# A planner's longer assumed landings, an earlier release, a second stack buffer, and a paced first attention

## The chip, the cores and the metric

The kernel runs on one core of a Trainium2 chip. The metric is the device time of one execution in microseconds (us); several runs give a median. A core has TensorE (PE, matrix products on a 128 x 128 array), VectorE (DVE), ScalarE (ACT), GpSimd (POOL) and SyncE (SP, which issues most DMAs here). Each engine takes its instructions in the order in which the program lists them, and engines wait for each other through semaphores.

## The reference

For each of 4 batches with N = 12480 rows of C = 128, 32 learned rows `I` attend to the batch, and the batch then attends to the 32 results. A feed-forward layer with a leaky ReLU follows on all 49920 rows.

```python
h = mab(I, x)                       # 32 rows per batch: the first attention
y = mab(x, h)                       # every row of x attends to h: the second attention
# mab(q, kv): s = scale * q @ kv.T; a = softmax(s); return a @ kv
t = y @ w_in                        # 128 -> 2048
g = maximum(0.01 * t, t)
out = g @ w_out                     # 2048 -> 128
```

## The kernel before

**Tiles.** A batch is cut into six full groups of 2048 rows and a remainder of 192 (`GROUPS`, remainder `RG`). A full group gives four tiles of 512 rows; the remainders of two batches make one pair tile of 384, which stands after the first four tiles of batches 1 and 3 (`PAIR_AT`). There are 98 tiles. The first two and the last are written in a fixed order; the 95 between (`work`) are planned.

**What a tile needs.** The second attention of a row is a vector `a` of 32 weights, so `y @ w_in` is `a @ (h @ w_in)`, and the kernel keeps `h @ w_in` (`hw`) instead of `y`. All operands of the feed-forward part are split into a high and a low part, and three products of parts stand for one exact one. A tile has 16 chunks of 128 hidden columns. Per chunk there are three first products of 32 rows of the array (`a` times `hw`), a ReLU on ScalarE (`ghi`), the low part on VectorE or, in its far form, on GpSimd (`glo`), and three second products in four row groups, all of the latter through `quarter` (L988). Products of four row groups run beside each other. The linear part of the leaky ReLU is added in chunk 13 (`LINEAR`), where `A4`, the tile's `a`, is read for the last time; the four partial sums are gathered and added after chunk 15 (`gather`).

**How `a` gets there.** `second(b, g)` makes the second attention of a group: scores on the array, then transpose and maximum (DVE), subtraction (POOL), exponential (ACT), sums (DVE), product (POOL) and a last transpose (DVE, L837) into `aT`. It runs for one group after another, in the order 0, 1, remainder, 2 to 5, with at most four full groups ahead. `stack` takes a group's `aT`, writes its high part with ACT (L856) and its low part with POOL (L863) into the one buffer `both`, and copies it with DMAs (L878) into the `A4` buffers of its four tiles, four DMAs of 128 KB for each (24 small ones for a pair tile). There are three `A4` buffers.

**The next batch.** When the first product of a batch's first tile is planned, `begin` starts the first attention of the next batch: `first_scores` (loads of x by 32 x 32 blocks, `xc`, 16 DMAs a group; transposes; scores, L372; `running` keeps a running maximum, L406) and `first_values` (loads of rows, `xr`, four DMAs a group; products, L535). Sums (L605) and the summary `h` (L624) follow, then `expand_weights` (L752). Batch 1's begins earlier, in the fixed part, with its loads and its remainder.

**What sets the order.** From `quads[0] = True` (L1183) on, a planner writes the instruction order. It keeps a clock per engine and a time per row group, adds assumed costs (`RELU`, `LOW`, `QUARTER`) and, for what a DMA brings, `LANDED` = 2300 ns after its issue, and emits whatever could start first by these numbers. The lanes (stack, stores, second attention, values, scores) ask for an engine and a time. On PE a lane waits until it is 9 us old (`OLD`), or until two are ready and one is 3 us old, or until the rows would be idle; on the other engines a lane gives way to feed-forward work until it is 15 us late (`PATIENCE`). First products may run at most ten chunks ahead (`GB`). None of this changes what waits on the chip, only the order.

Of the kernel before, what the change touches and what calls it, by code (L numbers as in the profile page):

```python
# [9 lines left out]
F32 = mybir.dt.float32  # L10
F32R = mybir.dt.float32r
# [8 lines left out]
def induced_attention_then_leaky_ffn(  # L20
# [63 lines left out]
    QUICK = 2  # L84
    TURN = 4
    A4_BUFS = 3
    XR = 9
    GB = 10
    SLOT = 868.0
    QUARTER = 231.6  # L90
    SIGNAL = 35.0
    DRAINED = 200.0
    TURNED = 200.0
    LANDED = 2300.0
    RELU, LOW, COPIED, ADDED, BLOCKS = 599.0, 690.0, 585.0, 685.0, 700.0
    FAR_HIGH, FAR_LOW, FAR_SUM = 611.0, 1291.0, 1291.0
    EARLY, PREFER, YIELDING, PATIENCE = 1200.0, 0.0, 200.0, 15000.0
    OLD, PAIRED, IDLE, HURRY, TOGETHER = 9000.0, 3000.0, 300.0, 9000.0, 3
    LINEAR = NF - 3
    debt = [0]  # L100

    const = ctx.enter_context(tc.tile_pool(name="const", bufs=1))
# [237 lines left out]
    def load_rows(b, g, q):  # L340

        _, J, K = GROUPS[g]
        n = min(K, 4)
        t = sb.tile([P, 4, C], F32, tag="xr", name="xr", bufs=XR)
        src = rows_of(b, g).rearrange("(p k) c -> p k c", k=K)
        nc.sync.dma_start(t[: 32 * J, :n, :], src[:, 4 * q : 4 * q + n, :])  # L346
        xr[b, g, q] = t
        landed[b, g, q] = spent(SP, 490.0) + LANDED

    def load_blocks(b, g, j0, nj):  # L350

# [103 lines left out]
    def first_scores(b):  # L455
# [12 lines left out]
            more()  # L468
        if not quads[0]:
            yield from idle(4)  # L470
        for g in [RG, *range(RG)]:
            _, J, K = GROUPS[g]
            w = 32 * K
            if g == RG:
                xT[b, g] = t = sb.tile([P, J, w], F32, tag="xTr", name="xTr", bufs=2)
            else:
                yield from until(lambda: len(ring) < RING)
                ring.add((b, g))
                xT[b, g] = t = sb.tile([P, J, w], F32, tag="xT", name="xT", bufs=RING)
            at = 0.0  # L480
            for j in range(J):
                if g == RG:
                    if j:
                        continue
                    blk, at = blocks[RG, 0, 3]
                    yield from new(DVE, at)
                    nc.vector.transpose(
                        t.rearrange("p j w -> p (j w)"),
                        blk[:, : J * K, :].rearrange("p n c -> p (n c)"),
                    )  # L490
                else:
                    blk, at = blocks[g, j - j % 2, 2]
                    yield from new(DVE, at)
                    blk = blk[:, (j % 2) * K : (j % 2 + 1) * K, :]
                    nc.vector.transpose(t[:, j, :], blk.rearrange("p n c -> p (n c)"))  # L495
                at = spent(DVE, BLOCKS, at)
                yield from old(HEAVY)
                if j % 2 or g == RG:
                    yield from new(SP, at)
                    more()  # L500
            yield from new(PE, at)
            sp = aux_ps("s1_ps")
            for j in range(J):
                columns_product(sp, indT, b, g, j)
            at = on_array("c", 875.0 if g != RG else 120.0, at, taken[0])
            if quads[0]:
                rest = running(b, g, sp, at)
                for got in rest:
                    if got[0] == PE:
                        break  # L510
                    yield got
                middles.append(carried(got, rest))
            else:
                yield from running(b, g, sp, at)
                yield from old()
# [260 lines left out]

    def second(b, g, eng=None):
        eng = eng or nc.gpsimd
        yield from until(lambda: g == RG or sum(q != RG for _, q in aT) < 4)
        if (b, g) != (0, 0):  # L780
            yield from new(PE, landed.get((b, "h"), 0.0))
        hT = hw[b][0]
# [59 lines left out]
    def stack(tiles_, eng=None):  # L842
# [3 lines left out]
        for _, parts in tiles_:  # L846
            for b, g, *_ in parts:
                if (b, g) not in at:
                    at[b, g] = sum(32 * GROUPS[q][2] for _, q in at)
        when = max(landed.get("both", 0.0), *(landed.get((b, g, "aT"), 0.0) for b, g in at))  # L850
        yield from new(ACT, when)
        both = sb.tile([P, 2, TOK], F32R, tag="both", name="both", bufs=1)
        ahi, alo = both[:, 0, :], both[:, 1, :]
        for (b, g), o in at.items():
            _, J, K = GROUPS[g]
# [12 lines left out]
        yield from old()  # L868
        for t, parts in tiles_:
            yield from until(lambda: len(A4) < A4_BUFS)  # L870
            a4 = sb.tile([P, 2, TOK], F32R, tag="A4", name="A4", bufs=A4_BUFS)
            to = 0
            for b, g, js in parts:
                w, o = 32 * GROUPS[g][2], at[b, g]
                for j in js:
                    yield from new(SP, when)
                    for r in range(4):
                        nc.sync.dma_start(  # L878
                            a4[32 * r : 32 * r + 32, :, to : to + w].bitcast(F32),
                            both[32 * j : 32 * j + 32, :, o : o + w].bitcast(F32),  # L880
                        )
                        landed["A", t] = landed["both"] = spent(SP, 640.0, when) + LANDED
                    to += w
                    yield from old()
            A4[t] = a4
# [3 lines left out]
    def quick(t):  # L889
# [11 lines left out]
        mx = sb.tile([P, 4], F32, tag="mx", name="qmx")  # L901
        nc.vector.tensor_reduce(out=mx, in_=sv, op=ALU.max, axis=AX.X)
        if not qys:
            qys.append(sb.tile([P, QUICK, 4, M], F32, tag="both", name="qy", bufs=1))
        y = qys[0][:, t]
        nc.vector.tensor_tensor(
            out=y, in0=sv, in1=mx.unsqueeze(2).broadcast_to([P, 4, M]), op=ALU.subtract
# [194 lines left out]
    with tc.manual_schedule():  # L1102
# [134 lines left out]
        def gather(t, r, ready):  # L1237
# [30 lines left out]
                add(ACT, ready, COPIED, copied, lambda: (t, 0) in parts_of)  # L1268
            else:
                add(ACT, ready, COPIED, copied, lambda: not parts_used[0])  # L1270
            if r == 3:
                del A4[t]

        def products(t, f, r):
            parts, n = spans(t)
# [60 lines left out]
        def go(r, kind, start):  # L1336
# [37 lines left out]
            if last:  # L1374
                product_of[r] = 0
                turn_of[r] += 1
                if min(turn_of) > i:
                    del live[t, f]
                if f == NF - 1:
                    gather(t, r, at)  # L1380

# [130 lines left out]
```

## Time and profile before

| | us |
|---|---|
| runs | 1601.34, 1604.66, 1604.69 |
| median of the runs | 1604.66 |
| profiled execution: time | 1606.44 |
| profiled execution: span | 1604.7 |
| PE busy | 1565.6 |
| DVE, ACT, POOL busy | 1084.6, 1080.4, 1179.3 |

The span is the time from the first to the last profiled instruction; about 1.7 us lie around it. The fixed part ends at about 100 us. Batch 1's first tile begins at about 452 us, batch 2's at about 855 us. PE counts as busy while any of its row groups runs, so the number of products in a stretch tells more than its busy time. The granted clock is the share of full speed that the array was given.

### The profile page before, as it was taken

Reading aid. Unit: us, or ns where it says so; the run is one execution under the profiler, and the core shown is the slowest. Engines: PE = TensorE matmul, PEld = TensorE weight load, DVE = VectorE, ACT = ScalarE, POOL = GpSimd, SP = SyncE. Lnnn points to the kernel's source line nnn. Section 1 sums busy time; section 2 is a strip of 40 time slices with the busy share of each in tenths; the row PEclk is TensorE's granted clock in tenths of the full one; section 3 lists DMA queues with packets and bytes.
Section 4 is the critical chain, followed back from the end, with each engine's and each line's share of the span. In section 5 each row is a group of like instructions: output and inputs, shape, how many; then the busy total and the mean of one; then the engine's idle time right before and its main releaser. Section 6 shows DMA issues by size and latency. Waiting matters only on the chain.

```text
span 1604.7 us, 60005 instructions
## 1 busy us (share of the span) xinstructions
PE 1565.6 (98%) x25047; PEld 1360.7 (85%) x25047; DVE 1084.6 (68%) x1914; ACT 1080.4 (67%) x1957; POOL 1179.3 (73%) x1227
## 2 busy tenths in 40 slices
PE   7989999999999999999999999999999999999998
PEld 5658878899997876889999877789898899999996
DVE  6667886665666867666666876566666677666665
ACT  6446657777775655667777566677777777777774
POOL 2028716999998255699999458999999957778773
PEclk9899999999999999999999999999999999999999
DMA  7155653223254557323234667233233233232231
GB/s 266 16 115 98 126 140 74 50 56 62 35 109 70 101 103 151 82 55 61 48 62 93 109 125 159 60 64 58 46 70 58 37 67 63 55 65 53 57 61 21
DMA packets 400704, 128.49 MB, mean 80 GB/s; under 512 B 373136, under 2 KB 375600, under 8 KB 400432
## 3 DMA queue, kind: packets, MB, share of 16 engines
q1 hardware_dynamic: 399328, 124.50, 38.7%
q8 instruction: 197, 3.23, 0.8%
q14 instruction: 75, 0.61, 0.1%
q10 hardware_dynamic: 1104, 0.15, 0.1%
HBM read 48.94 MB, written 25.56 MB: 46 GB/s over the span
## 4 chain that ended last, share of the span: by engine, by line
PE 89%; SPq 4%; DMA 4%; DVE 2%; issue 1%; ACT 1%; POOL 0%; ACTq 0%; DVEq 0%; POOLq 0%
PE bank L988 83%; PE bank L372 2%; DMA xr<-in_x_dram 2%; SPq L878 2%; SPq L357 1%; PE bank L1018 1%; PE bank L535 1%; DVE glo L978 1%; DMA raw<-in_moe_w_in_dram 1%; SPq L346 0%; DMA A<-both 0%; POOL glo L1218 0%; ACT ghi L975 0%; PE bank L406 0%; DMA out_dram<-osb 0%
## 5 line engine op out<-in xcount | busy, mean ns | idle before, releaser
L988 PE MATMUL bank<-ghi,w_hi 32*128 32x512 f32 (+1 forms) x6080 | 1221.3, 393 | 4.8 <-ACT ghi L975 4.8
L988 PE MATMUL bank<-ghi,w_lo 32*128 32x512 f32 (+1 forms) x6080 | 1214.6, 392 | 0.0
L988 PE MATMUL bank<-glo,w_hi 32*128 32x512 f32 (+1 forms) x6080 | 1213.7, 392 | 0.0
L988 PE MATMUL bank<-A,hwhi 32*128 32x512 f32 (+1 forms) x3394 | 1051.6, 392 | 9.1 <-ACT g L975 3.6
L978 DVE SCALAR_TENSOR_TENSOR glo<-bank,ghi 128x512 fp32r<-128x512 f32 (+1 forms) x1052 | 697.3, 682 | 362.9 <-ACT ghi L975 345.3
L988 PEld LDWEIGHTS bank<-ghi,w_hi 32*128 32x128 f32 x6080 | 775.4, 184 | 42.9 <-ACT ghi L975 6.0
L988 PEld LDWEIGHTS bank<-glo,w_hi 32*128 32x128 f32 x6080 | 770.0, 184 | 35.2 <-issue 9.8
L988 PEld LDWEIGHTS bank<-ghi,w_lo 32*128 32x128 f32 x6080 | 773.4, 184 | 31.0 <-issue 5.8
L975 ACT ACTIVATE ghi<-bank 128x512 fp32r<-128x512 f32 (+1 forms) x1052 | 611.5, 598 | 217.4 <-PE bank L988 187.6
L1218 POOL TENSOR_TENSOR glo<-g,ghi 128x512 fp32r<-128x512 f32 (+1 forms) x516 | 668.1, 1295 | 41.3
L988 PE MATMUL bank<-A,hwlo 32*128 32x512 f32 (+1 forms) x1697 | 621.6, 390 | 0.0
L988 PEld LDWEIGHTS bank<-A,hwhi 32*128 32x128 f32 x3394 | 569.1, 184 | 38.1 <-DVE glo L978 7.3
L975 ACT ACTIVATE g<-bank 128x512 f32<-128x512 f32 (+1 forms) x516 | 308.6, 598 | 210.2 <-PE bank L988 174.3
L1216 POOL CAST ghi<-g 128x512 fp32r<-128x512 f32 (+1 forms) x516 | 316.4, 613 | 135.6 <-ACT g L975 96.0
L988 PEld LDWEIGHTS bank<-A,hwlo 32*128 32x128 f32 x1697 | 302.5, 184 | 6.2 <-issue 1.4
L1261 POOL TENSOR_TENSOR part<-part 128x512 f32<-128x512 f32 (+1 forms) x95 | 123.0, 1295 | 96.3 <-DVE part L1250 93.3
L1250 DVE TENSOR_TENSOR part<-bank,part 128x512 f32<-128x512 f32 (+1 forms) x190 | 129.8, 685 | 64.2 <-PE bank L988 42.8
L1244 ACT COPY part<-bank 128x512 f32<-128x512 f32 (+1 forms) x190 | 110.4, 583 | 18.1 <-PE bank L988 14.9
L1037 DVE STREAM_TRANSPOSE osb<-part 128x512 f32<-128x512 f32 (+1 forms) x95 | 66.6, 701 | 11.2 <-POOL part L1261 10.5
L826 POOL TENSOR_TENSOR y<-y,sm 128x512 f32<-128x512 f32 (+1 forms) x27 | 25.4, 941 | 32.0 <-DVE sm L822 17.2
L495 DVE STREAM_TRANSPOSE xT<-xc 128x512 f32<-128x512 f32 x72 | 47.4, 689 | 1.3 <-DMA xc<-in_x_dram 1.3
L863 POOL TENSOR_TENSOR both<-aT,both 128x512 fp32r<-128x512 f32 x24 | 31.1, 1296 | 20.9 <-DMA xr<-in_x_dram 12.5
(120 smaller groups left out, 632.5 us busy)
## 6 DMA issues: line engine op xcount, KB each, us to landing
A<-both SPq DMA_DIRECT2D x376, 128.0 KB, 2.4
xr<-in_x_dram SPq DMA_DIRECT2D x96, 256.0 KB, 4.6
out_dram<-osb SPq DMA_DIRECT2D x382, 64.0 KB, 2.2
xc<-in_x_dram SPq DMA_DIRECT2D x288, 64.0 KB, 2.9
raw<-in_moe_w_in_dram SPq DMA_DIRECT2D x4, 512.0 KB, 6.6
raw<-in_moe_w_out_dram SPq DMA_DIRECT2D x4, 512.0 KB, 6.8
A<-both SPq DMA_DIRECT2D x48, 16.0 KB, 1.8
out_dram<-osb SPq DMA_DIRECT2D x48, 8.0 KB, 1.8
```

What stands on the lines that cost most here:

```text
L372: nc.tensor.matmul(dst, lhsT, rhs, start=True, stop=True)
L495: nc.vector.transpose(t[:, j, :], blk.rearrange("p n c -> p (n c)"))
L878: nc.sync.dma_start(a4[32 * r : 32 * r + 32, :, to : to + w].bitcast(F32), both[32 * j : 32 * j + 32, :, o : o + w].bitcast(F32),)
L975: nc.scalar.activation(ghi[:, :n], ph[:, :n], AF.Relu)
L978: nc.vector.scalar_tensor_tensor(out=glo[:, :n], in0=ph[:, :n], scalar=0.0, in1=ghi[:, :n].bitcast(F32), op0=ALU.max, op1=ALU.subtract,)
L988: nc.tensor.matmul(dst, w[32 * r : 32 * r + 32], x[32 * r : 32 * r + 32], start=start, stop=stop, tile_position=(32 * r, 0),)
L1037: nc.vector.transpose(osb[:, :n], total[:, :n])
L1216: nc.gpsimd.tensor_copy(ghi[:, :n], g[:, :n])
L1218: nc.gpsimd.tensor_tensor(out=glo[:, :n], in0=g[:, :n], in1=ghi[:, :n].bitcast(F32), op=ALU.subtract)
L1244: nc.scalar.copy(part[:, :n], po[:, :n])
L1250: nc.vector.tensor_tensor(out=part[:, :n], in0=po[:, :n], in1=part[:, :n], op=ALU.add)
L1261: nc.gpsimd.tensor_tensor(out=total[:, :n], in0=total[:, :n], in1=part[:, :n], op=ALU.add)
```

## The change

`LANDED` goes from 2300 to 3800 ns, with 3000 more for the row loads (`xr`). The slot of `A4` is given up when all row groups have passed chunk 13, instead of when the last partial sum is gathered, and a new load of `A4` is planned no earlier than that read. `both` gets a second buffer, and the planner's time for it is that of the stack before last. For the space, `xr` has 7 buffers instead of 9. In the first attention, group number n (the remainder is 0) is not started before n x 38 us after the beginning (`PACE`). In the planned part the second attention runs at most two full groups ahead instead of four (`STOCK`).

```diff
@@ -84,19 +84,20 @@
     QUICK = 2
     TURN = 4
     A4_BUFS = 3
-    XR = 9
+    XR = 7
     GB = 10
     SLOT = 868.0
     QUARTER = 231.6
     SIGNAL = 35.0
     DRAINED = 200.0
     TURNED = 200.0
-    LANDED = 2300.0
+    LANDED = 3800.0
     RELU, LOW, COPIED, ADDED, BLOCKS = 599.0, 690.0, 585.0, 685.0, 700.0
     FAR_HIGH, FAR_LOW, FAR_SUM = 611.0, 1291.0, 1291.0
     EARLY, PREFER, YIELDING, PATIENCE = 1200.0, 0.0, 200.0, 15000.0
     OLD, PAIRED, IDLE, HURRY, TOGETHER = 9000.0, 3000.0, 300.0, 9000.0, 3
     LINEAR = NF - 3
+    PACE, STOCK = 38000.0, 2
     debt = [0]
 
     const = ctx.enter_context(tc.tile_pool(name="const", bufs=1))
@@ -345,7 +346,7 @@
         src = rows_of(b, g).rearrange("(p k) c -> p k c", k=K)
         nc.sync.dma_start(t[: 32 * J, :n, :], src[:, 4 * q : 4 * q + n, :])
         xr[b, g, q] = t
-        landed[b, g, q] = spent(SP, 490.0) + LANDED
+        landed[b, g, q] = spent(SP, 490.0) + LANDED + 3000.0
 
     def load_blocks(b, g, j0, nj):
 
@@ -468,9 +469,11 @@
             more()
         if not quads[0]:
             yield from idle(4)
-        for g in [RG, *range(RG)]:
+        began = now[0]
+        for n, g in enumerate([RG, *range(RG)]):
             _, J, K = GROUPS[g]
             w = 32 * K
+            yield from until(lambda: not quads[0] or now[0] >= began + n * PACE)
             if g == RG:
                 xT[b, g] = t = sb.tile([P, J, w], F32, tag="xTr", name="xTr", bufs=2)
             else:
@@ -776,7 +779,7 @@
 
     def second(b, g, eng=None):
         eng = eng or nc.gpsimd
-        yield from until(lambda: g == RG or sum(q != RG for _, q in aT) < 4)
+        yield from until(lambda: g == RG or sum(q != RG for _, q in aT) < (STOCK if quads[0] else 4))
         if (b, g) != (0, 0):
             yield from new(PE, landed.get((b, "h"), 0.0))
         hT = hw[b][0]
@@ -847,9 +850,10 @@
             for b, g, *_ in parts:
                 if (b, g) not in at:
                     at[b, g] = sum(32 * GROUPS[q][2] for _, q in at)
-        when = max(landed.get("both", 0.0), *(landed.get((b, g, "aT"), 0.0) for b, g in at))
+        when = max(landed.get(("both", 1), 0.0), *(landed.get((b, g, "aT"), 0.0) for b, g in at))
         yield from new(ACT, when)
-        both = sb.tile([P, 2, TOK], F32R, tag="both", name="both", bufs=1)
+        landed["both", 1] = landed.get(("both", 0), 0.0)
+        both = sb.tile([P, 2, TOK], F32R, tag="both", name="both", bufs=2)
         ahi, alo = both[:, 0, :], both[:, 1, :]
         for (b, g), o in at.items():
             _, J, K = GROUPS[g]
@@ -868,6 +872,7 @@
         yield from old()
         for t, parts in tiles_:
             yield from until(lambda: len(A4) < A4_BUFS)
+            when = max(when, landed.get("A4", 0.0))
             a4 = sb.tile([P, 2, TOK], F32R, tag="A4", name="A4", bufs=A4_BUFS)
             to = 0
             for b, g, js in parts:
@@ -879,7 +884,7 @@
                             a4[32 * r : 32 * r + 32, :, to : to + w].bitcast(F32),
                             both[32 * j : 32 * j + 32, :, o : o + w].bitcast(F32),
                         )
-                        landed["A", t] = landed["both"] = spent(SP, 640.0, when) + LANDED
+                        landed["A", t] = landed["both", 0] = spent(SP, 640.0, when) + LANDED
                     to += w
                     yield from old()
             A4[t] = a4
@@ -901,7 +906,7 @@
         mx = sb.tile([P, 4], F32, tag="mx", name="qmx")
         nc.vector.tensor_reduce(out=mx, in_=sv, op=ALU.max, axis=AX.X)
         if not qys:
-            qys.append(sb.tile([P, QUICK, 4, M], F32, tag="both", name="qy", bufs=1))
+            qys.append(sb.tile([P, QUICK, 4, M], F32, tag="both", name="qy", bufs=2))
         y = qys[0][:, t]
         nc.vector.tensor_tensor(
             out=y, in0=sv, in1=mx.unsqueeze(2).broadcast_to([P, 4, M]), op=ALU.subtract
@@ -1268,8 +1273,6 @@
                 add(ACT, ready, COPIED, copied, lambda: (t, 0) in parts_of)
             else:
                 add(ACT, ready, COPIED, copied, lambda: not parts_used[0])
-            if r == 3:
-                del A4[t]
 
         def products(t, f, r):
             parts, n = spans(t)
@@ -1376,6 +1379,9 @@
                 turn_of[r] += 1
                 if min(turn_of) > i:
                     del live[t, f]
+                    if f == LINEAR:
+                        del A4[t]
+                        landed["A4"] = at
                 if f == NF - 1:
                     gather(t, r, at)
 
```

## Rows read from the trace of the kernel before

**Rows 1.** The page's engine totals: busy us (share of the span) xinstructions.

```profile
PE 1565.6 (98%) x25047; PEld 1360.7 (85%) x25047; DVE 1084.6 (68%) x1914; ACT 1080.4 (67%) x1957; POOL 1179.3 (73%) x1227
```

**Rows 2.** L988 on PE, quiet stretches: length, PE busy (xproducts), granted clock, DMA share, GB/s.

```profile
1320.00:1340.00 20.00, 20.00 (x348) 1.00 0.19 37
...
1160.00:1180.00 20.00, 19.07 (x329) 1.00 0.42 80
```

**Rows 3.** The same view for the four holes, and one piece of the second.

```profile
104.00:116.00 12.00, 7.71 (x76) 0.72 0.63 126
564.00:576.00 12.00, 8.37 (x96) 0.72 0.30 59
632.00:644.00 12.00, 6.33 (x72) 0.72 0.87 219
956.00:964.00 8.00, 2.87 (x32) 0.79 0.87 163
568.00:572.00 4.00, 3.04 (x28) 0.50 0.12 19
```

**Rows 4.** The same view for two longer stretches; then L372 and L535 in one.

```profile
480.00:520.00 40.00, 35.19 (x572) 1.00 0.42 70
200.00:260.00 60.00, 53.44 (x819) 1.00 0.49 119
...
200.00:260.00 60.00, 3.20 (x24) 1.00 0.49 119
...
200.00:260.00 60.00, 3.24 (x96) 1.00 0.49 119
```

**Rows 5.** Who waited for whom: us in total, times, longest.

```profile
ACT both L856 <- DMA out_dram<-osb: 14.0, 2, 9.6
ACT both L856 <- DMA A<-both: 12.5, 5, 5.0
```

**Rows 6.** Timelines of SyncE and of ScalarE: start, us, instruction [idle before it].

```profile
563.15 2.46 SPq L878 DMA_DIRECT2D A<-both  x4
...
567.79 0.62 ACT L856 CAST both<-aT 128x512 fp32r<-128x512 f32 x1 [4.42 <-DMA out_dram<-osb]
```

**Rows 7.** DMA issues by line: xcount, KB each, median us from issue to landing.

```profile
A<-both SPq DMA_DIRECT2D x376, 128.0 KB, 2.4
xr<-in_x_dram SPq DMA_DIRECT2D x96, 256.0 KB, 4.6
```

**Rows 8.** The chain of work that ended last: start, us, what.

```profile
132.90 0.99 PE bank L372 x8
...
222.92 1.07 PE bank L372 x8
...
277.85 0.42 PE bank L624 x2
282.08 0.99 PE bank L372 x8
...
632.72 4.54 DMA xr<-in_x_dram
...
1002.59 0.99 PE bank L372 x8
...
1035.68 0.42 PE bank L624 x2
```

**Rows 9.** Timeline of SyncE: start, us, issues.

```profile
499.85 16.96 SPq L878 DMA_DIRECT2D A<-both  x24
...
1274.27 18.34 SPq L878 DMA_DIRECT2D A<-both  x24
```

**Rows 10.** Timelines of VectorE and GpSimd in the second attention: start, us, instruction.

```profile
283.89 0.69 DVE L800 TENSOR_REDUCE mx<-y 128x16 f32<-128x512 f32 x1
...
320.50 1.04 POOL L826 TENSOR_TENSOR y<-y,sm 128x512 f32<-128x512 f32 x1
...
410.61 0.23 DVE L837 STREAM_TRANSPOSE aTr<-y 96x64 f32<-96x64 f32 x1
```

## Prediction, made before the change was run

> **What bounds the kernel now.** I read the engine totals first [rows 1]: TensorE is busy 98% of the span, so idle time elsewhere matters only where it reaches TensorE. "Busy" hides much, though: four row groups work side by side, and the engine counts as busy while one of them runs. So the second view is the number of feed-forward products (L988) by stretch. Undisturbed, the array starts 348 in 20 us [rows 2], 17.4 per us, or 57.5 ns each. A lone interruption (one attention score) leaves 329: 19 products, 1.1 us, against 0.99 us of its own work in the chain (the 132.90 row of [rows 8]); so the turn to another tiling costs about 0.1 us. Where far more is missing, the array starved.
>
> Four holes stand out [rows 3]. At 17.4 per us, 104 to 116 us should hold 209 products and has 76; 564 to 576 has 96 of 209; 632 to 644 has 72 of 209; 956 to 964 has 32 of 139. The granted clock shows that a hole costs twice: at 568 to 572, right after the array stood idle, it is 0.50, the lower of the two levels (1.2 against 2.4 GHz), and the products that do run take longer. Longer, thinner losses are in [rows 4]: 480 to 520 has 572 of 696, 200 to 260 has 819 of 1044, part of which is other array work.
>
> The third view, who waited for whom, gives the causes. ScalarE's copy into the stacked high part (L856) waited 12.5 us for the DMAs that read the previous stack and 14.0 us in two more waits put down to a store's landing [rows 5]. The timelines show that these two are the same wait: the four reads of the old stack are issued on SyncE from 563.15, and the copy starts at 567.79, just as the last can have landed [rows 6]; the store was only issued next. The ReLUs written behind the copy start only after it, and then the array. Holes 1 and 2 and the loss at 480 are this wait. Hole 3 is another: the array stands before the values of the first attention until rows of x have landed; the chain has 4.54 us of xr landing at 632.72 [rows 8]. Hole 4, at the same point of the next batch's burst, I take to be alike. The planner assumed 2.3 us after issue, and the median over the run is 4.6, against 2.4 for the A transfers [rows 7].
>
> **Two buffers for the stacked parts.** The copy then overwrites the stack before last, whose reads were issued a group of four tiles earlier. A tile is about 243 products, 14 us, so that is over 50 us old: the wait goes. What returns, missing products times 57.5 ns: hole 1, 133 products, 7.6 us, of which I take 6.0, because the hand-over to the planned part also has to fill the array's lead; hole 2, 113, 6.5 us, less 0.6 for a small interruption, 5.9; the loss at 480, 124, 7.1 us, less some 2.6 for the score, value and maximum work in it, 4.5. Sum 16.4 us. Next late at 480 is the pair tile itself, whose 24 small transfers take SyncE 16.96 us [rows 9]; the second such pair takes 18.34 us at 1274 and sits beside a quiet array, so I charge nothing for it unless the stack comes late (below). Paying with two xr buffers costs nothing: the first attention keeps at most five loads outstanding, and in the setup only the eighth weight tile comes to a slot that another one held, the first, which is read long before. Without that cover a load would wait one group, as it does at hole 3.
>
> **Longer assumed landings.** They only move instructions in the written order: values of the first attention go behind products that can run. Hole 3: 137 missing, 7.9 us, less 1.5 of its own values and maxima, 6.4 (values take 3.24 us for 96 products, 1.1 per group of 32 [rows 4]). Hole 4: 107, 6.2 us, less 1.1 of values, 5.1. Sum 11.5 us. The array gets other work in that time because the rows are then ordered 6.8 us after issue, beyond the median. For A the assumption grows by 1.5 us; nothing waits for it while three A buffers are in turn, so zero, with 0 to 1 us at the hand-over.
>
> The Trainium skill speaks against this part: "DMA: Bandwidth & Descriptors", section "Anatomy of one DMA — SWDGE (gpsimd) path", gives a DMA a constant 2.0 us plus its bytes over 436 GB/s, on another issuing path. By it 128 KB would take an estimated 2.3 us, 256 KB 2.6 us, the old assumption was right and this part would be worth nothing. The A transfers' median agrees; the xr median does not, and the measurement decides.
>
> **A let go at its last read.** The slot is free at the end of chunk 13, not 15, and a chunk of a tile is 14/16 = 0.9 us: its load is ordered 1.7 us earlier. Hidden, as the load has two tiles to land; zero.
>
> **Pacing of the first attention, stock of two.** Before, the five steps from the score at 132.90 to that at 222.92 came at 18 us each [rows 8]. An issue takes SyncE 0.62 us (4 in 2.46 us, [rows 6]) to 0.76 us (24 in 18.34 us, [rows 9]). A group has 16 xc and 4 xr loads, some 13 us, and a tile 4 A transfers and 4 stores, 5 us. At 18 us a group needs 13 + 6.5 us: SyncE is full. At 38 us it needs 13 + 14, 70%. So the bursts thin out, and of the thin losses part returns: 200 to 260 misses 225 products, 12.9 us, less 3.2 of scores, 3.2 of values and some 2 of maxima and turns, so 4 to 5 us. The third batch's burst has the same work in the same manner, so I double it and take half, 4.5 us; bounds 0 and 9. The cost: work that shared an interruption will stand alone more often. At 0.1 us a turn and some 20 more, 2 us (0 to 5).
>
> The pacing also **moves the end of each batch's first attention**, and this is the step that I trust least. The planned part starts at 100 us; the sixth full group may not start before 100 + 6 x 38 = 328. Transposes and the wait for the array bring its score to about 341, where it was 222.92. From the last score to the end of the summary (L624) it took 54.9 us in the first batch and 33.1 us in the third (1002.59 to 1035.68) [rows 8], so the summary comes at 374 to 396 instead of 278. Then the second attention runs one group after another, and each is held up at GpSimd, which is full of low parts, twice: from the maxima at 283.89 to the final product at 320.50 are 36.6 us [rows 10], in which GpSimd does only two steps of 1 us for it. That is some 15 us for each of the two, the planner's patience. The third group in line, the 192-row remainder that the pair tile needs, was finished at 410.61, 128.5 us after the first score of that chain at 282.08. Moved, it is finished at 374 + 4 + 128 = 506 to 528. The pair's transfers need 17 us more and then a landing, 525 to 547; before, they were issued from 499.85 to 516.81 and the array was just short of them. The array will be some 8 us ahead of the old times and has a lead of ten chunks, 9 us, so it runs dry at about 511 to 517. It would lack 8 to 36 us. But when it lacks products the low parts stop and GpSimd comes free, so one or two of the 15 us waits shrink; I take 8 us and 2 us of lower clock, 10. In the third batch the planned interval is about 25 us longer, and I charge 2. Bounds 0 and 40 in all.
>
> **Sum** against the profiled execution: 1606.44 us with a span of 1604.7. Returned: 16.4 + 11.5 + 4.5 = 32.4. Given back: 2 + 10 + 2 = 14. Net 18.4 us. The median of the runs shown is 1604.66, 0.1% under the profiled one; taken from it, 1586.3 us.
>
> **Rivals.** (1) The paced chain is in time: the second attention reaches the remainder sooner, and nothing is given back at the pair. Then 1586.3 - 12 = 1574; with all thin losses and the whole of hole 1 back as well, 1568. For it: the hold-up is the planner's choice and not GpSimd's own time of 2 us a group. Against: from 282 it met a full GpSimd, and the moved chain falls into the same kind of stretch. (2) The longer landings bring nothing: holes 3 and 4 are then a backlog in SyncE's queue, which the new order meets again. The 11.5 us stay lost, and 1598 results. Against: the last link before the values in the chain is a landing of 4.54 us, not an issue. The constant landing on the page of the Trainium skill named above would give the same time. (3) Slower: the late second attention costs at every pair its full waits. The mechanism is the 15 us waits at GpSimd; it decides from the point where the pair's two stalls pass 30 us together, that is, with the remainder finished at 528 and no easing: 36 + 8 of clock at the first, half of that at the second, 44 + 22 = 66 against the 30 returned: 1641; with some easing, about 1615. (4) The pacing gives back just what the waits return: 1602 to 1608. That the change does not do what it says is part of (2): the copy's wait can't stay, since its two releasers are reads of one buffer.
>
> **Chances.** Forecast (1579 to 1594) 0.48; (1) 0.22; (2) 0.12; (4) 0.07; (3) 0.11. Range 1567 to 1604: it leaves out (3) and the far ends, and takes in both bounds of the pair. The likeliest one's own range is 1579 to 1594. A measurement of this kernel can tell about 0.2%, 3.2 us. Faster by more 0.82, within 0.07, slower by more 0.11.
>
> **What would show it.** Right: no wait of L856 over 1 us; no xr landing in the chain at the first attention's values; 104 to 116 and 564 to 576 with over 170 products; SyncE with pauses in the bursts. For the pair: the array starved at about 505 to 530 with the wait put down to A, and the remainder's last transpose (L837) after 500. Wrong: the array full through that stretch (rival 1), or a hole at each batch's first tile, which would mean that even the first group of the second attention comes too late.

## The result and the profile after

The changed kernel takes **1584.32 us** (median of 4 runs, 1584.06 to 1585.30) against 1603.45 us (1601.34 to 1604.69) for the kernel before: ratio 0.9883, 95% interval 0.9866 to 0.9900, 19.1 us less. The forecast was 18.4 us less, 1586.3. The profiled span went from 1604.7 to 1582.3 us; 3 of these 22.4 us are there because the profiled run of before lay that far above its median. The mean granted clock rose from 0.986 to 0.994.

The sum came out nearly right, but not by its parts. The experiments show that the end of the waits for xr was credited to the wrong edit.

The engine totals of the page, which answer to [rows 1], and GpSimd's busy tenths in 40 slices of the span:

```profile
PE 1560.1 (99%) x25047; PEld 1357.9 (86%) x25047; DVE 1193.6 (75%) x2096; ACT 1080.0 (68%) x1957; POOL 840.7 (53%) x863
...
POOL 2127971566411399998311399977899843110100
```

The count on TensorE is the same. GpSimd lost 364 instructions and VectorE gained 182: 334 low parts are made on GpSimd where 516 were (L1223 against L1218), and the planner now gives the others to VectorE. Over the span VectorE is busy 75% and GpSimd 53%, so on average both have room for it.

Products (the quarter matmul, now L993) in the same windows as [rows 3] and [rows 4]: length, TensorE busy (xproducts), granted clock, DMA share, GB/s.

```profile
104.00:116.00 12.00, 9.40 (x116) 0.86 0.75 147
564.00:576.00 12.00, 9.82 (x162) 1.00 0.63 111
632.00:644.00 12.00, 11.07 (x192) 1.00 0.63 110
956.00:964.00 8.00, 8.00 (x144) 1.00 0.59 107
480.00:520.00 40.00, 38.38 (x666) 1.00 0.43 75
200.00:260.00 60.00, 56.72 (x934) 1.00 0.47 90
```

Holes 2, 3 and 4 are closed (162 for 96, 192 for 72, 144 for 32). Hole 1 is closed only in part: 116 where 76 were and 209 have room. At 480 the count flatters the change: the pair tile, whose products have 192 or 384 columns instead of 512, begins sooner, and 162 of the 666 products are such narrow ones, where 25 of the 572 were. Counted by columns it is 601 for 556, which is 2.6 us returned. Others of these windows flatter the change too, since paced attention work has moved out of them. A fairer count takes every stretch apart: the products started in it at 57.4 ns each (those of the pair tile by their columns), the spans of the interruptions by other array work, from the product before to the product after, and the rest, which is what the array missed. Undisturbed stretches show a rest of some 0.3 us in 20. Single rows move by up to 0.6 us with the side to which an interruption at an edge is counted; the sum does not.

| stretch, us | missed before | missed after | returned | forecast for it |
|---|---|---|---|---|
| 100 to 140 (hole 1) | 9.1 | 6.4 | 2.7 | 6.0 |
| 140 to 480 | 7.8 | 6.2 | 1.6 | 2.25 (pacing) |
| 480 to 680 (loss at 480, holes 2 and 3, first pair) | 18.3 + 4.1 standing at values | 9.4 | 13.0 | 16.8 - 10 |
| 880 to 1000 (hole 4) | 7.4 + 3.9 standing at values | 3.6 | 7.7 | 5.1 + 2.25 |
| 1000 to 1520 (second pair in it) | 8.7 | 9.5 | -0.8 | -2 |
| 680 to 880 | 2.5 | 3.1 | -0.6 | 0 |
| interruptions, 79 before and 86 after | | | -1.2 | -2 |
| sum | | | 22.4 | 18.4 |

Who waited for whom: us in total, times, longest. This is all that is left for the copy (now L860), where [rows 5] had 26.5 us of DMA waits, and all of the products' waits for A:

```profile
ACT both L860 <- DVE aT L840: 7.6, 2, 6.4
...
PE bank L993 <- DMA A<-both: 3.1, 1, 3.1
```

The longer wait lies at the hand-over. ScalarE's timeline and TensorE's there: start, us, instruction, idle before it.

```profile
105.16 0.62 ACT L860 CAST both<-aT 128x512 fp32r<-128x512 f32 x1 [6.41 <-DVE aT L840]
...
106.33 0.49 PE L993 MATMUL bank<-ghi,w_hi 32*128 32x512 f32 x1 [3.11 <-DMA A<-both]
```

The copy no longer waits for the old stack; it waits for the transposed tile that it is to copy. The next lateness stood right behind the one removed. What this wait costs is tested under "Closing hole 1".

The values (L538) wait for no landing of xr now, 7.0 us before. In all, TensorE stands idle 3.9 us after the first 96 us, 21.1 before.

Three rows answer to [rows 9] and [rows 10]: the remainder's last transpose and the pair tile's transfers in the first batch, and the transfers in the third.

```profile
L840 DVE STREAM_TRANSPOSE aTr<-y x1: 230/230/230, 464.9 to 464.9; 96x64 f32<-96x64 f32 x1
...
488.81 19.40 SPq L883 DMA_DIRECT2D A<-both  x28
...
1243.90 19.49 SPq L883 DMA_DIRECT2D A<-both  x28
```

The remainder is done at 464.9 us (410.61 before). I had expected 506 to 528.

### The profile page after: what moved, and what is told of

It reads as the page before. It is cut to its first block, busy times and chain, and to the rows that moved or that the text cites. A ratio compares the mean times of both kernels' runs of the same rounds, so it can differ in the third digit from the quotient of the medians.

```text
span 1582.3 us, 59604 instructions
## 1 busy us (share of the span) xinstructions
PE 1560.1 (99%) x25047; PEld 1357.9 (86%) x25047; DVE 1193.6 (75%) x2096; ACT 1080.0 (68%) x1957; POOL 840.7 (53%) x863
## 3 DMA queue, kind: packets, MB, share of 16 engines
q1 hardware_dynamic: 399328, 124.50, 39.2%
## 4 chain that ended last, share of the span: by engine, by line
PE 93%; DVE 3%; POOL 1%; ACT 1%; DMA 1%; issue 0%; SPq 0%; DVEq 0%; POOLq 0%; ACTq 0%
PE bank L993 86%; PE bank L373 3%; PE bank L1023 2%; PE bank L538 1%; DVE glo L983 1%; POOL glo L1223 1%; DMA xr<-in_x_dram 0%; PE bank L407 0%; POOL ghi L1221 0%; PE bank L671 0%; ACT ghi L980 0%; DVE cv_a L202 0%; DMA A<-both 0%; ACT xT L677 0%; PE bank L755 0%
## 5 line engine op out<-in xcount | busy, mean ns | idle before, releaser
L993 PE MATMUL bank<-ghi,w_hi 32*128 32x512 f32 x6080 | 1216.6, 392 | 3.2 <-DMA A<-both 3.1
L993 PE MATMUL bank<-glo,w_hi 32*128 32x512 f32 x6080 | 1219.6, 391 | 0.0
L993 PE MATMUL bank<-ghi,w_lo 32*128 32x512 f32 x6080 | 1215.1, 391 | 0.0
L993 PE MATMUL bank<-A,hwhi 32*128 32x512 f32 (+1 forms) x3394 | 1038.5, 391 | 2.4 <-DVE glo L983 1.4
L983 DVE SCALAR_TENSOR_TENSOR glo<-bank,ghi 128x512 fp32r<-128x512 f32 (+1 forms) x1234 | 815.3, 683 | 266.5 <-ACT ghi L980 243.9
L980 ACT ACTIVATE ghi<-bank 128x512 fp32r<-128x512 f32 (+1 forms) x1234 | 716.4, 598 | 269.7 <-PE bank L993 227.2
L993 PEld LDWEIGHTS bank<-glo,w_hi 32*128 32x128 f32 x6080 | 784.9, 183 | 37.4 <-issue 11.1
L993 PEld LDWEIGHTS bank<-ghi,w_hi 32*128 32x128 f32 x6080 | 779.7, 183 | 37.3 <-ACT ghi L980 4.4
L993 PEld LDWEIGHTS bank<-ghi,w_lo 32*128 32x128 f32 x6080 | 784.3, 183 | 31.8 <-issue 8.5
L993 PE MATMUL bank<-A,hwlo 32*128 32x512 f32 (+1 forms) x1697 | 616.0, 389 | 0.0
L993 PEld LDWEIGHTS bank<-A,hwhi 32*128 32x128 f32 x3394 | 562.2, 183 | 29.8 <-issue 5.2
L1223 POOL TENSOR_TENSOR glo<-g,ghi 128x512 fp32r<-128x512 f32 (+1 forms) x334 | 432.4, 1295 | 26.8
L993 PEld LDWEIGHTS bank<-A,hwlo 32*128 32x128 f32 x1697 | 298.9, 184 | 8.5 <-issue 2.7
L980 ACT ACTIVATE g<-bank 128x512 f32<-128x512 f32 (+1 forms) x334 | 200.1, 599 | 143.1 <-PE bank L993 122.8
L1221 POOL CAST ghi<-g 128x512 fp32r<-128x512 f32 (+1 forms) x334 | 204.9, 613 | 140.0 <-ACT g L980 74.0
L807 POOL TENSOR_TENSOR y<-y,mx 128x512 f32<-128x512 f32 (+1 forms) x27 | 25.4, 940 | 63.3 <-DVE mx L803 52.0
```

The costliest lines, as they stand in the source:

```text
L980: nc.scalar.activation(ghi[:, :n], ph[:, :n], AF.Relu)
L983: nc.vector.scalar_tensor_tensor(out=glo[:, :n], in0=ph[:, :n], scalar=0.0, in1=ghi[:, :n].bitcast(F32), op0=ALU.max, op1=ALU.subtract,)
L993: nc.tensor.matmul(dst, w[32 * r : 32 * r + 32], x[32 * r : 32 * r + 32], start=start, stop=stop, tile_position=(32 * r, 0),)
L1221: nc.gpsimd.tensor_copy(ghi[:, :n], g[:, :n])
L1223: nc.gpsimd.tensor_tensor(out=glo[:, :n], in0=g[:, :n], in1=ghi[:, :n].bitcast(F32), op=ALU.subtract)
```

## The experiments

Three parts of the change, the second buffer (with its seven xr buffers), the longer landings and the pacing, were each made alone (in the kernel before) and taken back alone (from the changed kernel). The kernel before, timed beside them, took 1603.14 to 1603.82 us.

**Two buffers, alone and taken back.**

```diff
-        both = sb.tile([P, 2, TOK], F32R, tag="both", name="both", bufs=1)
+        both = sb.tile([P, 2, TOK], F32R, tag="both", name="both", bufs=2)
```

with `XR` 7 and `landed["both", 1]` as in the change, in the kernel before:

> The kernel before with the second stack buffer alone (and seven xr buffers). Theory: holes 1 and 2 and the loss at 480 close, holes 3 and 4 stay: 11 to 16 us less, 1588 to 1593 us. Rival: the copy only waited in a queue that SyncE could not empty in time, and the pair of waits is replaced by waits for A on the array: 1599 to 1604 us.

Measured: 1599.25 us, ratio 0.9969 (0.9955 to 0.9984). That is the rival's time, but no wait of the array for A is there. Its products (L989) in the old windows, and two of its first attention's values:

```profile
104.00:116.00 12.00, 10.38 (x132) 0.86 0.59 114
564.00:576.00 12.00, 11.76 (x201) 1.00 0.45 69
...
480.00:520.00 40.00, 38.38 (x668) 1.00 0.41 69
...
214.51 0.43 PE L535 MATMUL bank<-xr,ay 128*32 128x128 f32 x8 [1.93 <-DMA xr<-in_x_dram]
...
624.45 0.43 PE L535 MATMUL bank<-xr,ay 128*32 128x128 f32 x8 [1.58 <-DMA xr<-in_x_dram]
```

At hole 2 the edit does what was forecast: 105 products more in the window, and the copy waits for no DMA. At 480 there are 96 more, but 124 of the 668 are narrow ones of the pair tile; by columns it is 616 for 556, 3.5 us. Yet the kernel gains only 4.5 us. The waits for xr grew from 7.0 to 11.9 us, and 500 to 540 still misses 7.1 us.

One rival for these longer waits is the price of the edit. With seven xr buffers SyncE's loads of rows wait for the values to give a buffer back; the kernel before shows no such wait. SyncE's own waits (us in total, times, longest), in this kernel and in the changed one:

```profile
SPq L346 <- PE bank L535: 10.1, 6, 3.1
...
SPq L347 <- PE bank L538: 9.5, 4, 5.3
```

The number of xr buffers was not changed alone, so its share of the time is not known.

The reverse, in the changed kernel (one buffer, `XR` 9):

> The changed kernel with one stack buffer again (and nine xr buffers), all else kept. Theory: the copy's wait was the larger part of the gain, 16.4 us in the prediction, of which the two traces leave some 12 (2.8 us at 100 to 140 us, about 9 between 480 and 620); it comes back, 1594 to 1599 us, with waits of L860 for reads of the stack of several us. Rival: the pacing empties SyncE, the reads land when the planner thinks, and the second buffer is not needed: 1584 to 1587 us.

Measured: 1596.93 us, 0.9957 (0.9942 to 0.9972), 12.6 us over the changed kernel. Of the copy's waits for DMAs 9.3 us came back, nearly all of it the first one:

```profile
106.12 0.62 ACT L860 CAST both<-aT 128x512 fp32r<-128x512 f32 x1 [8.89 <-DMA A<-both]
```

The array's idle time rose only from 3.9 to 7.5 us, so most of the 12.6 us is no wait of the array.

**Longer landings, alone and taken back.**

```diff
-    LANDED = 2300.0
+    LANDED = 3800.0
...
-        landed[b, g, q] = spent(SP, 490.0) + LANDED
+        landed[b, g, q] = spent(SP, 490.0) + LANDED + 3000.0
```

> The kernel before with the longer assumed landings alone. The prediction's term: holes 3 and 4 close, 11.5 us less, 1590 to 1594 us. Rival (2) of the prediction, which the run without pacing favours, since it kept xr waits of 1.4 to 1.7 us on the array: with SyncE full the loads are issued late, not only landed late, so the new order meets the wait again: 1599 to 1606 us.

Measured: **1620.59 us, slower**, 1.0100 (1.0082 to 1.0118), past both ranges. Waits for xr fell from 7.0 to 2.6 us, and the old windows of holes 3 and 4 are as full as in the changed kernel:

```profile
632.00:644.00 12.00, 11.34 (x188) 1.00 0.66 122
956.00:964.00 8.00, 8.00 (x144) 1.00 0.61 103
```

So in these two places the edit does what was forecast. But the copy's waits rose to 30.8 us, and products worth 5 us were lost by 170 us already, 10 by 230. All engines in 130 to 230 us: length; TensorE, weight load, VectorE, ScalarE, GpSimd busy (xinstructions); clock; DMA share; GB/s. First this kernel, then the kernel before:

```profile
130.00:230.00 100.00, 98.32 (x1431) 77.55 (x1430) 89.25 (x176) 58.92 (x113) 17.46 (x16) 1.00 0.62 122
```

```profile
130.00:230.00 100.00, 99.99 (x1572) 80.29 (x1568) 84.60 (x168) 61.05 (x116) 59.28 (x62) 1.00 0.63 123
```

TensorE stood still only 1.7 us, but started 141 instructions fewer, and GpSimd was busy 17 us for 59. The thin loss is not a wait that a view names.

> The changed kernel with the old assumed landings (2300 ns, nothing more for xr). The prediction's term: holes 3 and 4 return, 11.5 us, 1596 us. Rival: the pacing loads rows a group, 38 us, ahead of their use, so they have landed whatever the planner assumes, and this part is idle beside it: 1583 to 1587 us.

Measured: 1592.90 us, 0.9926 (0.9907 to 0.9945), between the two. No wait for xr at all, though the landings are the old ones. Some 5 of the 8.6 us over the changed kernel are lost between 1260 and 1320: GpSimd makes the second pair's low part at 1256.7 for 1233.8, and its A transfers start at 1258.4 for 1243.9.

**Pacing, alone and taken back.**

```diff
+    PACE, STOCK = 38000.0, 2
...
+            yield from until(lambda: not quads[0] or now[0] >= began + n * PACE)
...
-        yield from until(lambda: g == RG or sum(q != RG for _, q in aT) < 4)
+        yield from until(lambda: g == RG or sum(q != RG for _, q in aT) < (STOCK if quads[0] else 4))
```

> The kernel before with the pacing and the stock of two alone (one stack buffer, nine xr buffers, short landings). The sum of the prediction has only 4.5 us of thin losses for the pacing and 14 us given back: 1604 to 1613 us. The theory after the first four runs: a SyncE that is not full lets reads and rows land when the planner thinks, so pacing alone closes holes 2 to 4 and the loss at 480; only hole 1, before the pacing acts, stays: 1588 to 1597 us, with no xr wait on the array.

Measured: 1591.97 us, 0.9928 (0.9906 to 0.9950): **the largest single gain, 12 us**. No wait for xr is left. The copy's DMA waits stay, 16.7 us:

```profile
ACT both L859 <- DMA out_dram<-osb: 8.9, 1, 8.9
ACT both L859 <- DMA A<-both: 7.8, 4, 3.0
```

The stock of two was not tried alone. Pacing taken back from the changed kernel (`PACE` 0, stock still 2):

> The changed kernel with no pacing (stock of two kept). Theory: the bursts return with SyncE full, thin losses of 4 to 9 us come back, and 1 to 2 us of turns are saved: 1587 to 1592 us. Rival, the prediction's step on the pair tile: pacing costs 12 us at the two pairs, so without it the time is 1575 to 1581 us.

Measured: 1600.15 us, 0.9981 (0.9965 to 0.9997), past both ranges. The waits for xr are back, 6.7 us, at hole 3's old place, with the long landings in force:

```profile
633.51 0.43 PE L538 MATMUL bank<-xr,ay 128*32 128x128 f32 x8 [1.73 <-DMA xr<-in_x_dram]
634.31 0.43 PE L538 MATMUL bank<-xr,ay 128*32 128x128 f32 x8 [0.38 <-DMA xr<-in_x_dram]
636.11 0.65 PE L538 MATMUL bank<-xr,ay 128*32 128x128 f32 x8 [1.37 <-DMA xr<-in_x_dram]
```

SyncE's timeline of this kernel gives the reason: start, us, issues. The rows of x follow 6.26 us of xc issues, themselves queued without a pause:

```profile
619.04 3.46 SPq L1059 DMA_DIRECT2D out_dram<-osb  x4
622.55 6.26 SPq L358 DMA_DIRECT2D xc<-in_x_dram  x8
628.85 2.04 SPq L347 DMA_DIRECT2D xr<-in_x_dram  x4
630.98 2.45 SPq L883 DMA_DIRECT2D A<-both  x4
```

They were issued at 628.85, the values came to them at 632. Hole 3 of the kernel before has the same picture:

```profile
617.89 7.40 SPq L357 DMA_DIRECT2D xc<-in_x_dram  x8
625.39 3.40 SPq L878 DMA_DIRECT2D A<-both  x4
628.89 2.65 SPq L1054 DMA_DIRECT2D out_dram<-osb  x4
631.58 2.05 SPq L346 DMA_DIRECT2D xr<-in_x_dram  x4
```

Summed over 590 to 640 us, SyncE issues 48.7 of 50 us before, 49.1 with pacing taken back, 49.2 with longer landings alone; 40.2 with pacing alone, 39.9 in the changed kernel. In 130 to 170 it was 39.2 of 40 before and 26.2 after. With longer landings alone it is 26.4 there, so the loss of that kernel by 170 us is not a full SyncE.

**The deadline at the pair: pace 46.**

```diff
-    PACE, STOCK = 38000.0, 2
+    PACE, STOCK = 46000.0, 2
```

> The changed kernel with 46 instead of 38 us a group. The mechanism of the prediction's step on the pair tile: the summary of batch 1 comes some 48 us later than in the changed kernel, at about 423 us, the first group of the second attention at 440 to 455, the remainder at 515 to 530; batch 1's first tile and its pair tile starve, in batch 3 the pair tile: 15 to 30 us more, 1600 to 1615 us. Rival: the second attention runs fast enough while GpSimd has room, and nothing starves: 1582 to 1588 us.

Measured: 1617.66 us, 1.0082 (1.0067 to 1.0097), 33 us over the changed kernel and just past the expected range. In the first batch the summary comes at 428.9, and tiles at 452 to 455 wait for A. In the third the remainder is done at 1283.6 (1230.8 at pace 38), and the pair's transfers follow at once:

```profile
1285.64 21.52 SPq L883 DMA_DIRECT2D A<-both  x32
...
1292.75 1.76 PE L993 MATMUL bank<-A,hwhi 32*128 32x192 f32 x3 [2.40 <-DMA A<-both]
...
1300.33 0.52 PE L993 MATMUL bank<-A,hwhi 32*128 32x192 f32 x1 [5.39 <-DMA A<-both]
```

So the wait that I feared exists, but at 46 us a group and not at 38. The slices of the page show a lower clock there as well, and 1280 to 1320 misses 17.4 us. The changed kernel is not far from it: its third batch copies the pair's stack 0.1 us after the remainder's transpose, though the transfers start only 10 us after the low part (1233.8, 1243.9).

**The other side: pace 28, and the neighbour 36.** The same line with 28000 and 36000.

> The changed kernel with 28 instead of 38 us a group. Theory: what counts is that SyncE is not full; a group needs some 13 us of issues beside 10 us of tiles, 23 of 28, so the losses stay out: 1582 to 1587 us. Rival: wider spacing matters by itself (contention of transfers, VectorE), and half of the 16 us between no pacing and 38 us is lost: 1589 to 1594 us.

Measured: 1601.98 us, 0.9985 (0.9974 to 0.9996). The expectation fell, and the rival's range was passed too. The premise had failed: in 590 to 640 us SyncE issues 48.9 of 50 us at this pace, and 2.9 us of waits for xr are back, at 610 and 629. At 36 us a group it issues 41.5, at 38 us 39.9 and at 46 us 31.6, and nothing waits for xr. All engines in 140 to 310 us, pace 28 and then the changed kernel:

```profile
140.00:310.00 170.00, 168.11 (x2599) 140.49 (x2599) 137.11 (x257) 106.89 (x200) 66.72 (x68) 1.00 0.52 103
```

```profile
140.00:310.00 170.00, 170.00 (x2799) 144.81 (x2795) 132.90 (x236) 116.09 (x211) 106.33 (x110) 1.00 0.52 100
```

In this stretch it is the pattern of the longer landings alone: fewer products, more low parts on VectorE, GpSimd idle. Over the whole span GpSimd's share tells fast from slow in no way: it is busy 841 us in the changed kernel, 870 at pace 28 and 1008 at pace 36. I took the planner's margin (`EARLY`, by which it calls a low part due before its slot) for the cause, and ran pace 28 with it at zero:

```diff
-    EARLY, PREFER, YIELDING, PATIENCE = 1200.0, 0.0, 200.0, 15000.0
+    EARLY, PREFER, YIELDING, PATIENCE = 0.0, 0.0, 200.0, 15000.0
```

> 28 us a group, and the planner's margin for giving a low part to GpSimd lowered from 1200 ns to 0, so that it does so with less lead. Theory from the traces: at 28 us the array's lead is lost once, the planner then gives all low parts to VectorE (81% busy from 140 to 310 us, GpSimd 39%), which limits the array, so the lead does not come back. With the lower margin GpSimd takes more of them and half or more of the 18 us returns: 1584 to 1593 us. Rival: SyncE or the transfers limit at 28 us, and who makes the low parts is a consequence: 1598 to 1606 us.

Measured: 1607.87 us, 1.0026 (1.0015 to 1.0036). Early, it does what the theory says: GpSimd is busy 158 of the 170 us, TensorE starts 2796 instructions, and by 310 us most of the loss is gone (3.9 us behind the changed kernel, where pace 28 is 15). From there it falls back bit by bit, to 24 us at the end. The total therefore proves nothing about the cause.

> The changed kernel with 36 instead of 38 us a group: does the gain hang on one lucky order? If the pacing works by what it leaves free on VectorE and SyncE, 36 is close to 38: 1582 to 1589 us. If a small change of a constant reshuffles the order at random, anything up to 1602 us, the time at 28 us, may come.

Measured: 1585.90 us (1585.34 to 1586.36), 0.9886 (0.9867 to 0.9905), within 1.6 us of the changed kernel.

**How much an order scatters.** One constant that means nothing at this size, in the kernel before:

```diff
-    SIGNAL = 35.0
+    SIGNAL = 36.0
```

> The kernel before with one planner constant moved by 1 ns (the assumed signal, 35 to 36 ns), which means nothing by itself. If the planner's order is stable, the time is that of before within 4 us, 1599 to 1608 us. If orders scatter, it moves by more, and every single-edit difference of that size in these runs has to be read with that scatter.

Measured: 1614.37 us, 1.0066 (1.0046 to 1.0086): **11 us slower for 1 ns of an assumed signal time**. ScalarE's copy at hole 2 (its wait was 4.42 us in [rows 6]), and the array behind it:

```profile
570.22 0.62 ACT L856 CAST both<-aT 128x512 fp32r<-128x512 f32 x1 [7.60 <-DMA out_dram<-osb]
...
571.39 0.61 PE L988 MATMUL bank<-ghi,w_hi 32*128 32x512 f32 x2 [4.68 <-ACT ghi L975]
```

**Closing hole 1.** The planner places the first copy while its input is not ready. Telling it so, in the changed kernel:

```diff
         when = max(landed.get(("both", 1), 0.0), *(landed.get((b, g, "aT"), 0.0) for b, g in at))
+        when = max(when, 8000.0)
```

> The changed kernel with the first planned copy into the stack ordered no earlier than 8 us after the hand-over (later copies come later anyway). In the changed kernel this copy waits 6.4 us for aT, and the first ReLUs stand behind it, 3.1 us of idle array and a lower clock until 114 us. Theory: hole 1 closes further, 3 to 5 us less, 1579 to 1582 us, if the order behind it stays as good. Rival: the low parts or A limit there as well, or the later order gets worse: 1584 us or more.

Measured: 1602.32 us, 0.9992 (0.9981 to 1.0003), 18 us over the changed kernel. The copy at 104.06 us waits for nothing any more, yet 100 to 120 still misses 4.6 us for 5.5. So the copy's wait is not what holds hole 1 open. The array now waits for low parts, which VectorE makes after the second attention's transposes:

```profile
105.44 2.47 DVE L984 SCALAR_TENSOR_TENSOR glo<-bank,ghi 128x512 fp32r<-128x512 f32 x4
...
106.18 0.79 PE L994 MATMUL bank<-glo,w_hi 32*128 32x512 f32 x1 [2.33 <-DVE glo L984]
```

This is the rival. By 370 us the kernel is 6 us behind the changed one, and the second pair costs some 9 us more: the remainder is done at 1266.2 us (1230.8 in the changed kernel), and the pair's transfers follow at once, as at pace 46.

```profile
1267.49 22.35 SPq L884 DMA_DIRECT2D A<-both  x32
```

So a late pair looks possible at 38 us a group as well, when the order shifts, though no view names a wait of the array for A there.

No kernel of these beat the changed one.

## Why the forecast came out, step by step

**The copy's wait: mechanism right, 16.4 us not its worth.** The wait is absent in every kernel with two buffers and present in every one without. Of the three terms, hole 2 is right locally: alone, the edit brings 105 x 57.5 ns = 6.0 us there, for 5.9. The loss at 480 came back only in part, by columns 3.5 us alone and 2.6 in the changed kernel, for 4.5; I had counted narrow products of the pair tile as whole ones. Hole 1 was mis-sized, 2.7 us for 6.0: I allowed for the array's lead, and not for what stands next behind the old stack. That is the transposed tile, and with its wait gone as well the low parts on VectorE. And the three can't be added to the total, since alone the edit is worth 4.5 us. Nor was the price of two xr buffers nothing, as I had it: SyncE's loads wait 9.5 to 10.1 us for a buffer to be given back. What that costs was not tested.

**Longer landings: the step that failed.** I wrote that the values come later in the order and so find their rows, and gave 11.5 us for it. Holes 3 and 4 did close, but in the changed kernel the term isn't needed for it. With pacing and the old landings nothing waits for xr; with the new landings and no pacing, 6.7 us of waits are back. Alone the new landings do fill the two windows and leave 2.6 us of waits, but the order that they make is 17 us slower. What I had taken as rival (2), a backlog in SyncE's queue, is the cause of the waits: where SyncE issues 49 of 50 us (before, both unpaced single edits, pacing taken back, 28 us a group) values wait for rows that were issued late, and where it issues 32 to 43 (36, 38 and 46 us a group, pacing alone, one buffer, short landings) none does. The kernel with 1 ns more lies between, at 44.9, with 3.2 us of such waits, most of them in the next batch. The last link that I read, a landing of 4.54 us, hid an issue that came late. Beside the other two edits the part goes with a gain of 8.6 us, more than half of which is a later place of the second pair's low part and not its own mechanism.

By the Trainium skill's "DMA: Bandwidth & Descriptors", section "Anatomy of one DMA — SWDGE (gpsimd) path" (a constant 2.0 us and the bytes over 436 GB/s, on another issuing path), I had an estimate of 2.6 us for 256 KB. The changed kernel's median is 4.4 us with a SyncE that pauses, so the estimate stays too low. Its consequence, that this part is worth nothing, came nearer than my 11.5 us, for another reason.

**Pacing: wrong sign, as far as single times tell.** It stood in the sum at 4.5 - 2 - 12, a cost of 9.5. Alone it gains 12 us (with the stock of two), taken back it costs 16. I saw that SyncE was full (18 us a group for 13 + 6.5) and that at 38 us it would not be, and drew only half of thin losses from it. The step that was missing: holes 3 and 4 are the same full queue.

**The pair: mis-sized, mechanism real.** I charged 10 us for the first pair, with the remainder at 506 to 528. The summary came at 374.4, the early end of the 374 to 396 forecast, but the chain from its first score at 378.3 took 87 us to the remainder, not 128. I had carried over the waits of a full GpSimd. The row of slices shown above (40 slices of 39.6 us) has it at 4, 1 and 1 tenths from 396 to 514; that this room is what shortened the chain was not tested. 500 to 540 still misses 5.2 us, but about as much with no pacing, so it isn't lateness. Pace 46 shows that the deadline exists. That is rival (1) for this step, and rival (3)'s mechanism for a pace that was not chosen.

**A let go at its last read, and the turns.** The release was not tried alone. SyncE's A transfers wait for the array nearly as long as before (253.7 us in 74 waits, 248.9 in 67), and the array's own waits for A are 3.1 us, 1.6 before. Seven interruptions came more, 1.2 us, for some 20 and 2 us.

So two errors met: up to 11.5 us too much for the landings, and by the single times 21 to 25 too little for the pacing, less what the parts lose when they are added. That the sum was within 1 us of the measured difference is no proof of its terms; the forecast's sign rested on both named waits going, and they went.

**What stays open.** Single edits gave -4.5, +17 and -12 us, which add up to about nothing; undoing them cost 12.6, 8.6 and 16, which add up to 37. The gain was 19. One nanosecond gave 11 us, one useful line 18. So time differences of 10 to 15 us between these kernels cannot be put down to one edit; the waits in the traces can. Part of the gain does add up, in the array's idle time. TensorE in 96 to 1520 us: length, busy (xinstructions), clock, DMA share, GB/s, in the kernel before, with two buffers alone, with pacing alone and in the changed kernel:

```profile
96.00:1520.00 1424.00, 1403.17 (x23185) 0.99 0.40 79
...
96.00:1520.00 1424.00, 1407.78 (x23330) 0.99 0.40 79
...
96.00:1520.00 1424.00, 1415.56 (x23439) 1.00 0.41 79
...
96.00:1520.00 1424.00, 1420.37 (x23577) 1.00 0.41 80
```

The idle time falls by 4.6 us with the buffers, by 12.4 with the pacing and by 17.2 with the whole change, next to 4.5, 12 and 19 us of time. With the old landings in the changed kernel it is as short, 3.3 us for 3.6, so the longer landings are not needed for it. The losses go another way. With the 1 ns the array is idle 16.2 us, as little as with two buffers, and the time rises by 11; with the short landings it is idle 3.3 us, with the later first copy 6.2: there the time lies in stretches that start fewer products while no view names a wait. The stock of two, the release of A and the number of xr buffers were not tried alone. How much of the 19 us is a lucky order is not known, though pace 36 repeats it. Why orders with long landings alone or at pace 28 leave GpSimd idle was only argued.

## What to carry to other kernels

Before a landing is called slow, look at when it was issued and whether the issuing queue had a pause: a full queue is cured by spreading the loads, not by assuming a longer flight, and the spread ends where the next deadline starts (here 46 us a group was past it). In a kernel whose order a planner writes, judge an edit by the wait that it removes and by a neighbouring constant, never by one time. Where an in-order engine waits to overwrite a buffer, a second one takes the wait away, but expect the next late producer to stand right behind it, and see what the space was taken from.

## What the runs showed of the hardware that I had not expected

- Kernels in which the copy or the values wait some 7 us or more for a landing scatter from run to run: the highest time is over the lowest by 8.5 us (before, 21 runs), 8.8 (two buffers alone), 7.8 (no pacing), 5.2 (one buffer), 6.1 (pacing alone), 4.1 (1 ns more). With 3 to 4 us of such waits it is 2.0 (pace 28) and 3.4 (margin of zero), without them 0.7 to 2.4: 1.2 (changed), 1.0 (pace 36), 0.7 (pace 46), 2.4 (short landings, paced), 2.2 (first copy later). Longer landings alone are the exception, with 30.8 us of waits and 1.0 us. The kernels had 4 to 21 runs each, and that the waits cause the scatter is not shown.
- A queue that pauses hardly shortens the median landing of xr, 4.4 us for 4.6. What changed is when the loads were issued.
- The granted clock at hole 2 was 0.72 in [rows 3] and is 1.00 after, so the lower level came with the idle array and went with it.
